# A row layout in runs of 2 KB, loads of row tiles in pairs, and centring shared by VectorE and ScalarE, at the head of a fused attention and gated-MLP kernel

## Chip, cores, metric

One core of a Trainium2 chip. The metric is device time in microseconds (us); medians of several executions are given with their range. Engines: PE is TensorE, DVE is VectorE, ACT is ScalarE, POOL is GpSimd, SP is SyncE, which here only issues DMAs.

## The reference

```python
x  = A_x                                   # (1, 2048, 512) bf16
xn = layernorm(x)                          # over the last axis
q  = (xn @ wq) in 32 heads of 128
o  = softmax(q @ k_cache.T * 128**-0.5) @ v_cache     # 32 heads, 2048 keys
s  = o @ wo                                # (4096 -> 512)
g  = silu((relu(xn @ W_gate) * (xn @ W_up)) @ W_down) # 512 -> 1792 -> 512
out = x + s * g
```

## The kernel before

The program first computes `g`, in four Q blocks of 512 rows, then a long attention stage, then the last projection. The change touches the head of the first Q block only. There the rows are centred (the scale of the layernorm is folded in later), transposed by PE, copied to `xcT`, and multiplied by the first column blocks ("fc", 128 columns) of `W_gate` and `W_up`. The first fc blocks are done row tile by row tile ("small blocks": 4 matmuls of 128 columns for the gate and 4 for up), the others over all 512 rows ("full blocks").

```python
x_t   = x2.rearrange("(n p) d -> p n d", p=128)     # row n*128+p on partition p
out_t = out2.rearrange("(n p) d -> p n d", p=128)
# ... (cut)
FCS = [0, 2, 5, 9, FC]      # W_gate and W_up come in four pieces of fc blocks
HFC = 3                     # so many fc blocks go by row tile
load_x0(sp, 0); load_x0(act, 1)          # single row tiles, 128 KB, 1 KB runs
load_w(sp, Wg_sb, wg_src, sem_wg, 0)     # 256 KB, fc 0 and 1
load_w(act, Wu_sb, wu_src, sem_wu, 0)
load_x0(sp, 2); load_x0(sp, 3)
# pieces 1 of Wg, Wu; second 512 rows of x; pieces 2; pieces 3; third and fourth 512 rows; W_down
_wait(act, eps_tok)
warm_tok = sem_sq.sig(act.activation(sqv[:, 0, :], eps_sb[:], ACTF.Sqrt))   # loads the table
# ... (cut)
def head_center(n):
    atok = ln_aggr([n], ln_stats(n))          # DVE: bn_stats, bn_aggr
    _wait(dve, atok)
    return sem_ln4.sig(dve.tensor_scalar(xc_sb[:, n, :], x_sb[:, n, :], mv[:, n, 0:1], None,
                                         op0=ALU.subtract))
def head_transpose(n, ntok):                  # PE: 4 transposes, then ACT: copy to xcT
    # ... (cut)
def head_ln():
    c0 = head_transpose(0, head_center(0)); warm_mm(4)
    c1 = head_transpose(1, head_center(1))
    n2 = head_center(2); n3 = head_center(3)
    _wait(pe, c0); head_tile(0, 0); head_tile(0, 1)
    _wait(pe, c1); head_tile(1, 0); head_tile(1, 1)
    c2 = head_transpose(2, n2); head_tile(0, 2); head_tile(1, 2)
    # ... (cut)
warm_mm(18); head_ln()      # 18 matmuls on constants while the first loads are under way
```

In the full blocks of the first Q block, DVE also takes the statistics of the later rows of x, one tile per fc block, so it waits there for the later loads of x.

The softmax here doesn't subtract the row's maximum and nothing guards it: scores larger than these inputs give would overflow.

## Time and profile before

| | before |
|---|---|
| time, 6 runs (the prediction had the first 3, median 1286.01) | 1285.68 us (1285.48 to 1286.48) |
| span of the profiled run | 1284.4 us |
| first small block starts | 6.28 us |
| first matmul of the second Q block | 44.03 us |
| from there to the end | 1240.37 us |

Everything after the start of the second Q block is bound by PE. Two lines of the page of the kernel before show it, the busy times by engine and the chain of work that ended last, by engine:

```profile
PE 1279.1 (100%) x12050; PEld 836.4 (65%) x12050; DVE 380.5 (30%) x683; ACT 1002.2 (78%) x1111; POOL 13.2 (1%) x25
...
PE 98%; DVE 1%; ACT 0%; issue 0%; DMA 0%; ACTq 0%; DVEq 0%
```

The timeline of the kernel before, 3 to 7 us. Columns: start in us, busy us, engine, line, operation, output and input, and in brackets how long the engine had stood idle and for whom.

```profile
3.48 0.69 DVE L313 BATCH_NORM_STATS2 stats<-x_sb 128x6 f32<-128x512 bf16 x1 [3.48 <-DMA x_sb<-in_A_x_dram]
...
4.43 0.35 DVE L348 TENSOR_SCALAR xc_sb<-x_sb,mv 128x512 bf16<-128x512 bf16 x1
4.70 0.69 DVE L313 BATCH_NORM_STATS2 stats<-x_sb 128x6 f32<-128x512 bf16 x1
...
4.93 0.38 PE L358 MATMUL ps_acc<-ident,xc_sb 128*128 128x128 bf16 x4 [0.16 <-DVE xc_sb L348]
...
5.64 0.35 DVE L348 TENSOR_SCALAR xc_sb<-x_sb,mv 128x512 bf16<-128x512 bf16 x1
...
6.05 0.40 PE L358 MATMUL ps_acc<-ident,xc_sb 128*128 128x128 bf16 x4 [0.29 <-DVE xc_sb L348]
...
6.28 0.39 PE L410 MATMUL ps_r<-xcT,Wg_sb 128*128 128x128 bf16 x4
```

DVE begins when the first tile has landed, needs 1.2 us a tile, and PE, in order, does tile 1's transposes (6.05) before the first small block (6.28).

The same view at 19 to 22 us:

```profile
19.62 0.69 DVE L313 BATCH_NORM_STATS2 stats<-x_sb 128x6 f32<-128x512 bf16 x1 [0.78 <-DMA x_sb<-in_A_x_dram]
...
19.95 1.03 PE L512 MATMUL ps_r<-xcT,Wu_sb 128*128 128x512 bf16 x4
...
20.51 0.69 DVE L473 TENSOR_TENSOR hT<-gr_sb,ps_r 128x512 bf16<-128x512 bf16 x1
...
21.34 1.02 PE L508 MATMUL ps_r<-xcT,Wg_sb 128*128 128x512 bf16 x4 [0.37 <-DVE hT L473]
```

DVE stood 0.78 us for the third load of x; the product that frees PE's buffer slot came late, and PE's next full block began at 21.34, though the block before it needed PE only to 20.8 (19.95 plus four steps of 0.216).

The DMA view of the kernel before, DMAs in flight around 1 to 1.6 us: what, issuing queue, count, KB each, us from issue to landing.

```profile
Wu_sb<-in_B_W_up_dram ACTq DMA_DIRECT2D x1, 256.0 KB, 4.2
Wg_sb<-in_B_W_gate_dram SPq DMA_DIRECT2D x1, 256.0 KB, 3.9
x_sb<-in_A_x_dram ACTq DMA_DIRECT2D x1, 128.0 KB, 2.9
x_sb<-in_A_x_dram SPq DMA_DIRECT2D x1, 128.0 KB, 2.7
```

The windows view of the kernel before, for PE alone. Columns: stretch, its length, PE busy (instructions), granted clock, DMA share, GB/s.

```profile
1.36:4.77 3.41, 3.41 (x16) 1.00 0.91 248
4.77:8.19 3.42, 2.97 (x48) 1.00 1.09 330
```

Before a first change is recorded the clock column reads 1.00, but PE's pace is then half: the 18 warm-up matmuls took 4.00 us in all, 0.22 each, while eighteen of the same took 2.18 in a4_bridge below, after full speed had been granted. And the stretches are cut by the clock's own record: in this trace full speed was granted at 4.77 us, and the cuts lie there and 3.41 us to either side, the length of the shortest stretch in the changed kernel's record below.

### The profile page before, as it was taken

Reading aid. Unit: us, or ns where it says so; the run is one execution under the profiler, and the core shown is the slowest. Engines: PE = TensorE matmul, PEld = TensorE weight load, DVE = VectorE, ACT = ScalarE, POOL = GpSimd, SP = SyncE. Lnnn points to the kernel's source line nnn. Section 1 sums busy time; section 2 is a strip of 40 time slices with the busy share of each in tenths; the row PEclk is TensorE's granted clock in tenths of the full one; section 3 lists DMA queues with packets and bytes.
Section 4 is the critical chain, followed back from the end, with each engine's and each line's share of the span. In section 5 each row is a group of like instructions: output and inputs, shape, how many; then the busy total and the mean of one; then the engine's idle time right before and its main releaser. Section 6 shows DMA issues by size and latency. Waiting matters only on the chain.

```text
span 1284.4 us, 26956 instructions
## 1 busy us (share of the span) xinstructions
PE 1279.1 (100%) x12050; PEld 836.4 (65%) x12050; DVE 380.5 (30%) x683; ACT 1002.2 (78%) x1111; POOL 13.2 (1%) x25
## 2 busy tenths in 40 slices
PE   9999999999999999999999999999999999999998
PEld 5444466676666666666666666666666666666665
DVE  6433311112222222222222222222222222224355
ACT  3322399998888888888888888888888888888885
POOL 2100000000000000000000000000000000000000
PEclk9999999999999999999999999999999999999999
DMA  9600123332132332332322322233323322332212
GB/s 262 131 1 1 22 46 57 58 55 38 35 54 46 71 54 50 55 70 51 55 43 33 67 46 54 55 66 55 55 51 65 58 35 38 51 67 54 48 16 75
DMA packets 242033, 72.13 MB, mean 56 GB/s; under 512 B 227840, under 2 KB 241920, under 8 KB 241920
## 3 DMA queue, kind: packets, MB, share of 16 engines
q1 hardware_dynamic: 241248, 70.02, 29.6%
q8 instruction: 96, 1.57, 0.5%
q10 hardware_dynamic: 672, 0.39, 0.1%
q14 instruction: 17, 0.14, 0.0%
HBM read 32.77 MB, written 2.10 MB: 27 GB/s over the span
## 4 chain that ended last, share of the span: by engine, by line
PE 98%; DVE 1%; ACT 0%; issue 0%; DMA 0%; ACTq 0%; DVEq 0%
PE ps_acc L769 36%; PE ps_r L664 34%; PE ps_r L597 9%; PE ps_r L618 8%; PE ps_acc L531 3%; PE ps_r L508 3%; PE ps_r L512 3%; PE ps_r L803 1%; DVE stats L313 0%; PE ps_r L410 0%; DVE hT L473 0%; DMA x_sb<-in_A_x_dram 0%; DVE fin_tmp L811 0%; ACT gr_sb L467 0%; DVE x_sb L827 0%
## 5 line engine op out<-in xcount | busy, mean ns | idle before, releaser
L674 ACT ACTIVATE PT<-ps_r 128x1024 bf16<-128x1024 f32 x1024 | 952.5, 1054 | 167.7 <-PE ps_r L664 167.7
L769 PEld LDWEIGHTS ps_acc<-V_sb,PT 128*128 128x128 bf16 x8192 | 621.2, 98 | 241.9 <-ACT PT L674 3.5
L769 PE MATMUL ps_acc<-V_sb,PT 128*128 128x129 bf16 x8192 | 776.7, 220 | 0.0
L664 PE MATMUL ps_r<-QT_sb,KT_sb 128*128 128x512 bf16 x2048 | 754.1, 379 | 0.0
L691 DVE RECIPROCAL rz_sb<-ps_acc 128x4 f32<-128x4 f32 x127 | 23.3, 183 | 729.8 <-PE ps_acc L769 729.8
L664 PEld LDWEIGHTS ps_r<-QT_sb,KT_sb 128*128 128x128 bf16 x2048 | 195.0, 98 | 1.1 <-DVE QT_sb L608 0.4
L597 PE MATMUL ps_r<-xnT,Wq_sb 128*128 128x512 bf16 x512 | 130.9, 379 | 0.0
L618 PE MATMUL ps_r<-Wo_sb,OT_store 128*128 128x512 bf16 x448 | 114.6, 379 | 0.0
L608 DVE CAST QT_sb<-ps_r 128x512 bf16<-128x512 f32 x128 | 88.5, 692 | 48.1 <-PE ps_r L597 48.1
L597 PEld LDWEIGHTS ps_r<-xnT,Wq_sb 128*128 128x128 bf16 x512 | 49.9, 97 | 60.6 <-ACT PT L674 27.1
L694 DVE TENSOR_TENSOR Onorm<-ps_acc,rz_sb 128x512 bf16<-128x512 f32 x127 | 87.8, 691 | 4.4
L618 PEld LDWEIGHTS ps_r<-Wo_sb,OT_store 128*128 128x128 bf16 x448 | 43.8, 98 | 52.9 <-ACT PT L674 0.2
L631 DVE TENSOR_TENSOR s_acc<-s_acc,ps_r 128x512 f32<-128x512 f32 x96 | 66.0, 687 | 17.3 <-PE ps_r L618 17.3
L467 ACT ACTIVATE gr_sb<-ps_r 128x512 bf16<-128x512 f32 x55 | 32.2, 595 | 47.5 <-PE ps_r L508 47.0
L473 DVE TENSOR_TENSOR hT<-gr_sb,ps_r 128x512 bf16<-128x512 bf16 x55 | 37.7, 686 | 47.5 <-PE ps_r L512 41.2
L531 PE MATMUL ps_acc<-Wd_sb,hT 128*128 128x512 bf16 x224 | 49.2, 379 | 0.1
L508 PE MATMUL ps_r<-xnT,Wg_sb 128*128 128x512 bf16 x168 | 43.1, 379 | 0.0
L512 PE MATMUL ps_r<-xnT,Wu_sb 128*128 128x512 bf16 x168 | 43.1, 379 | 0.0
L531 PEld LDWEIGHTS ps_acc<-Wd_sb,hT 128*128 128x128 bf16 x224 | 21.8, 98 | 26.8 <-DVE g_sb L548 0.6
L539 ACT ACTIVATE sig_sb<-ps_acc 128x512 f32<-128x512 f32 x12 | 7.2, 597 | 29.5 <-PE ps_acc L531 29.5
L508 PEld LDWEIGHTS ps_r<-xnT,Wg_sb 128*128 128x128 bf16 x168 | 16.4, 98 | 19.8
L512 PEld LDWEIGHTS ps_r<-xnT,Wu_sb 128*128 128x128 bf16 x168 | 16.4, 98 | 19.8
(56 smaller groups left out, 184.7 us busy)
## 6 DMA issues: line engine op xcount, KB each, us to landing
V_sb<-in_A_v_cache_dram SPq DMA_DIRECT2D x32, 512.0 KB, 4.7
Wq_sb<-in_A_wq_dram SPq DMA_DIRECT2D x32, 128.0 KB, 2.5
Wo_sb<-in_A_wo_dram SPq DMA_DIRECT2D x8, 512.0 KB, 4.8
OT_store<-Onorm SPq DMA_TRANSPOSE x127, 2.5
Wd_sb<-in_B_W_down_dram SPq DMA_DIRECT2D x1, 1792.0 KB, 14.5
x_sb<-in_A_x_dram SPq DMA_DIRECT2D x3, 512.0 KB, 10.8
out_dram<-x_sb SPq DMA_DIRECT2D x6, 256.0 KB, 2.1
Wg_sb<-in_B_W_gate_dram SPq DMA_DIRECT2D x1, 640.0 KB, 10.3
```

Source lines behind the costliest of these rows:

```text
L473: dve.tensor_tensor(hT[par][:, fc, :], gr_sb[gk][:], u_ps, ALU.mult)
L508: ins = pe.matmul(g_ps, Wg_sb[:, c, fs], xT[:, c, xs], start=(c == 0), stop=(c == DC - 1))
L512: ins = pe.matmul(u_ps, Wu_sb[:, c, fs], xT[:, c, xs], start=(c == 0), stop=(c == DC - 1))
L531: ins = pe.matmul(ps_acc[:, jb, 0:D], hT[par][:, fc, j * 128:(j + 1) * 128], Wd_sb[:, fc, :], start=(fc == 0), stop=(fc == FC - 1))
L597: ins = pe.matmul(ps_r[:, bank, :], Wq_sb[b][:, c, :], xnT[:, c, qs], start=(c == 0), stop=(c == DC - 1))
L608: etok = sem_qpe.sig(dve.tensor_copy(QT_sb[b][:, qs], ps_r[:, bank, :]))
L618: ins = pe.matmul(ps_r[:, bank, 0:D], OT_store[g % 2][:, hh, n * 128:(n + 1) * 128], Wo_sb[g % 2][:, hh, :], start=(hh == 0), stop=(hh == ...
L631: dve.tensor_tensor(s_acc[:, n, :], s_acc[:, n, :], ps_r[:, bank, 0:D], ALU.add)
L664: ins = pe.matmul(ps_r[:, 2 * s + tt, :], KT_sb[h % 2][:, t * 128:(t + 1) * 128], QT_sb[h % 2][:, qs], start=True, stop=True)
L674: act.activation(PT[pb][:], ps_r[:, 2 * s:2 * s + 2, :], ACTF.Exp, scale=scale)
L694: dve.tensor_tensor(Onorm[ob][:], o_ap, rz_sb[:].to_broadcast([128, 4, Dh]), ALU.mult))
L769: ins = pe.matmul(o_ap, PT[pb][:, tt, j * 128:(j + 1) * 128], V_sb[vb][:, t, 0:VW], start=(t == 0 and j % 2 == 0), stop=(t == KT - 1 and j ...
```

## The change

The intent: longer runs for the loads of x, both engines at work on the centring, less waiting for late loads, and fewer small blocks. The core of the diff (later helpers and renamings cut):

```diff
-    x_t = x2.rearrange("(n p) d -> p n d", p=128)
-    out_t = out2.rearrange("(n p) d -> p n d", p=128)
+    x_t = x2.rearrange("(p n) d -> p n d", p=128)      # row p*16+n on partition p
+    out_t = out2.rearrange("(p n) d -> p n d", p=128)
-        HFC = 3
+        HFC = 2
-        load_x0(sp, 0)
-        load_x0(act, 1)
+        load_x0(0)                     # tiles 0,1 in one DMA: 2 KB runs, all on SP's queue
+        load_x0(1)                     # tiles 2,3
         load_w(sp, Wg_sb, wg_src, sem_wg, 0)
+        _wait(act, eps_tok)
+        sem_sq.sig(act.activation(sqv[:, 0, :], eps_sb[:], ACTF.Sqrt))
         load_w(act, Wu_sb, wu_src, sem_wu, 0)
-        load_x0(sp, 2)
-        load_x0(sp, 3)
 ... (pieces 1, second 512 rows of x, pieces 2)
+        load_xq(2)                     # third 512 rows of x, ahead of the last pieces
         load_w(sp, Wg_sb, wg_src, sem_wg, 3)
         load_w(sp, Wu_sb, wu_src, sem_wu, 3)
-        for Q in range(2, QB):
+        for Q in range(3, QB):
             load_xq(Q)
+        def center_act(n):
+            _wait(act, x0_tok[n // 2])
+            stok = sem_xa.sig(act.activation(xc_sb[:, n, :], x_sb[:, n, :], ACTF.Copy,
+                                             scale=-1.0 / D, accum_out=nmean[:, n, :]))
+            _wait(act, stok)
+            return sem_xa.sig(act.activation(xc_sb[:, n, :], x_sb[:, n, :], ACTF.Identity,
+                                             bias=nmean[:, n, :]))
         def head_ln():
-            c0 = head_transpose(0, head_center(0))
-            warm_mm(4)
-            c1 = head_transpose(1, head_center(1))
+            n0 = center_dve(0)
+            n1 = center_act(1)
+            p0 = head_tr(0, n0)
+            p1 = head_tr(1, n1)
+            warm_mm(3)
+            c0 = head_copy(0, p0, act)
+            stok = ln_stats(2)          # DVE: statistics of tile 2, then tile 1's copy
+            c1 = head_copy(1, p1, dve)
 ... (tile 2 centred by DVE, tile 3 by ACT; copies 2 by DVE, 3 by ACT; small blocks of fc 0 and 1;
      the statistics of tiles 1 and 3 come last)
```

More of the change, by code (lines that the diff above doesn't have):

```diff
@@ L142, in bass_recurrent_scan__mha_block_cached__glu_gated_reglu__prompt_kernel @@
         xcT = SB_([128, DC, NQ], BF16, "xcT")
+        nmean = SB_([128, 4, 1], F32, "nmean")
         r2 = SB_([128, 4, 1], F32, "r2")
@@ L157, in bass_recurrent_scan__mha_block_cached__glu_gated_reglu__prompt_kernel @@
         sem_x = [newsem(16) for _ in range(QB)]
-        sem_x0 = [newsem(16) for _ in range(4)]
+        sem_x0 = [newsem(16) for _ in range(2)]
         sem_wg = [newsem(16) for _ in range(4)]
@@ L224, in bass_recurrent_scan__mha_block_cached__glu_gated_reglu__prompt_kernel, with load_x0 @@
         x_tok = {}
-        def load_x0(eng, n):
-            x0_tok[n] = sem_x0[n].sig(eng.dma_start(x_sb[:, n:n + 1, :], x_t[:, n:n + 1, :]))
+        def load_x0(k):
+            x0_tok[k] = sem_x0[k].sig(
+                sp.dma_start(x_sb[:, 2 * k:2 * k + 2, :], x_t[:, 2 * k:2 * k + 2, :]))
         def load_xq(Q):
@@ L243, in bass_recurrent_scan__mha_block_cached__glu_gated_reglu__prompt_kernel @@
         load_w(sp, Wu_sb, wu_src, sem_wu, 2)
+        load_xq(2)
         load_w(sp, Wg_sb, wg_src, sem_wg, 3)
         load_w(sp, Wu_sb, wu_src, sem_wu, 3)
-        for Q in range(2, QB):
+        for Q in range(3, QB):
             load_xq(Q)
         sem_wd.sig(sp.dma_start(Wd_sb[:], B_W_down.rearrange("(c p) d -> p c d", p=128)))
-        _wait(act, eps_tok)
-        warm_tok = sem_sq.sig(act.activation(sqv[:, 0, :], eps_sb[:], ACTF.Sqrt))
         def issue_kt(h):
@@ L309, in ln_stats @@
             if n < 4:
-                _wait(dve, x0_tok[n])
+                _wait(dve, x0_tok[n // 2])
             elif n % 4 == 0:
@@ L342, in bass_recurrent_scan__mha_block_cached__glu_gated_reglu__prompt_kernel, with center_dve, head_tr @@
         xt_ready = {Q: [] for Q in range(QB)}
-        def head_center(n):
-            atok = ln_aggr([n], ln_stats(n))
-            _wait(dve, atok)
+        def center_dve(n):
+            _wait(dve, ln_aggr([n], ln_stats(n)))
             return sem_ln4.sig(
                 dve.tensor_scalar(xc_sb[:, n, :], x_sb[:, n, :], mv[:, n, 0:1], None, op0=ALU.subtract))
-        def head_transpose(n, ntok):
+        def center_act(n):
+            _wait(act, x0_tok[n // 2])
+            stok = sem_xa.sig(
+                act.activation(xc_sb[:, n, :], x_sb[:, n, :], ACTF.Copy, scale=-1.0 / D,
+                               accum_out=nmean[:, n, :]))
+            _wait(act, stok)
+            return sem_xa.sig(
+                act.activation(xc_sb[:, n, :], x_sb[:, n, :], ACTF.Identity, bias=nmean[:, n, :]))
+        def head_tr(n, ntok):
             tp_ps = acc_bf[n % 2]
@@ L359, in head_transpose, with head_copy @@
                                    xc_sb[:, n, c * 128:(c + 1) * 128], ident[:])
-            ptok = sem_tp.sig(ins)
-            src = tp_ps[:, 0:DC * 128].rearrange("p (c q) -> p c q", c=DC)
-            _wait(act, ptok)
-            acc_free[n % 2] = sem_xa.sig(act.copy(xcT[:, :, n * 128:(n + 1) * 128], src))
+            return sem_tp.sig(ins)
+        def head_copy(n, ptok, eng):
+            src = acc_bf[n % 2][:, 0:DC * 128].rearrange("p (c q) -> p c q", c=DC)
+            _wait(eng, ptok)
+            copy, sem = (act.copy, sem_xa) if eng is act else (dve.tensor_copy, sem_xt)
+            acc_free[n % 2] = sem.sig(copy(xcT[:, :, n * 128:(n + 1) * 128], src))
             return acc_free[n % 2]
@@ L373, in head_ln @@
         def head_ln():
-            c0 = head_transpose(0, head_center(0))
-            warm_mm(4)
-            c1 = head_transpose(1, head_center(1))
-            n2 = head_center(2)
-            n3 = head_center(3)
+            n0 = center_dve(0)
[6 more added lines that the diff above has]
+            c1 = head_copy(1, p1, dve)
+            _wait(dve, ln_aggr([2], stok))
+            n2 = sem_ln4.sig(
+                dve.tensor_scalar(xc_sb[:, 2, :], x_sb[:, 2, :], mv[:, 2, 0:1], None, op0=ALU.subtract))
+            n3 = center_act(3)
             _wait(pe, c0)
@@ L383, in head_ln @@
             head_tile(1, 0)
+            p2 = head_tr(2, n2)
+            c2 = head_copy(2, p2, dve)
             head_tile(1, 1)
-            c2 = head_transpose(2, n2)
-            head_tile(0, 2)
-            head_tile(1, 2)
+            p3 = head_tr(3, n3)
+            c3 = head_copy(3, p3, act)
             _wait(pe, c2)
             head_tile(2, 0)
-            c3 = head_transpose(3, n3)
             head_tile(2, 1)
-            head_tile(2, 2)
             _wait(pe, c3)
-            for fc in range(HFC):
-                head_tile(3, fc)
+            head_tile(3, 0)
+            head_tile(3, 1)
+            for n in (1, 3):
+                ln_aggr([n], ln_stats(n))
         half_slots = []
```

## The prediction

> **What bounds the kernel.** The page gives PE 1279.1 of 1284.4 us busy; the chain that ended last is 98% PE. By the windows view PE never idles from 38 us to the last ten. The change leaves that work as it is and can only move when PE gets through the first 38 us. There the timeline shows:
> - 0 to 6.28 us: warm-up and transposes; the first useful matmul (xcT, row tile 0) starts at 6.28. PE, in order, waited for tile 1: DVE takes the tiles in turn, 1.2 us each (statistics 0.69, aggregate 0.18, centring 0.35).
> - 6.28 to 12.18: 12 small blocks (0.445 us) and two transposes (0.22): 5.78 us of work in 5.90.
> - 12.18 to 37.97: 11 full blocks (1.73) and 28 down matmuls (0.216): 25.07 us of work in 25.79. Of the 0.72 lost, 0.5 is at 20.8, where DVE had stood 0.78 us for the third load of x (landed 10.8 us after issue) and freed a slot late; 0.2 at 37.8, where the first gate (r2h, table load 1.28, tanh 0.69, two DVE steps) frees its bank late.
>
> **What the change does.**
> - x in pairs, 2 KB runs, same bytes. The first pair lands near 3.5 us (before: 3.46 and 3.63); the second, now ahead of Wg, near 4.3. The third load of x goes ahead of the last 1.28 MB of weights: at the trace's 349 GB/s 3.7 us earlier, so DVE's wait goes.
> - ACT issues the first Wu load after table load and warm-up, near 2.2 us (was 1.16). It took 4.2 us to land; again so, it lands at 6.2 to 6.4, just when needed. [...] the trace agrees (from 4 to 5 us the queues show 62 and 52%), so Wu need not wait for all of SP's.
> - ACT centres tile 1 in two passes, estimated 0.6 us each from its 0.58 to 0.60 for 512 columns: done near 4.85, as tile 0. Both transposed by 5.4; copy ends near 6.0, first useful matmul 6.05: gain 0.2.
> - Tile 2's copy goes to DVE (estimated 0.69 from its PSUM reads; ACT 0.58), and one small block and one transpose less stand between its transpose and its use: 1.2 us needed, 0.9 covered, loses 0.3.
> - HFC 3 to 2: four small blocks (1.78) become one full (1.73), and an early wait for the second Wu piece goes: gains 0.15.
> - Two late statistics (1.7 us) fall where DVE has room.
> - Output writes become 2 KB for early pairs: off the chain.
>
> **Sum.** Start +0.2; tile-2 bubble -0.3; Wu late -0.15 (0 to 0.4); small blocks +0.15; wait at 20.8 +0.5; gate wait +0.2, since DVE is no longer behind: 0.6 us gained, carried to the end because PE is bound there.
>
> **Prediction: 1285.4 us, range 1284.7 to 1286.1** (before 1286.01, runs 0.8 apart). Chances: faster by over 2% 0.01; within 2% 0.98; slower 0.01.
>
> **What would show it.** Timeline: first small block near 6.05; a PE gap near 8.3 before tile 2's blocks; DVE never waiting for x after the start; no PE gap at 20 to 21 or at 37; the second Q block's first matmul 0.6 earlier than 44.03, all later work shifted alike.
>
> **What would make it wrong.** Reads with a 16 KB stride between partitions landing later than contiguous ones; Wu landing after 6.5; the accumulating ACT pass costing much over 0.6; DVE still behind, so the gate wait remains; exp and matmuls falling differently in step in the long stage.

Between 4 and 5 us the packets of SP's and ACT's queues took 52 and 62% of the 16 engines' time. The sum: its six terms (+0.2, -0.3, -0.15, +0.15, +0.5, +0.2) come to 0.6 us.

## More of the kernel before

The three sets of experiments ran on three chips (a runs, b runs, c runs); the kernel before, timed beside each, agreed within 0.05 us.

Wg was issued at 1.19 and landed near 5.1; the weights are there before PE wants them.

## The result, and the profile after

| | before | changed |
|---|---|---|
| time, 6 runs each | 1285.68 us (1285.48 to 1286.48) | 1287.67 us (1285.70 to 1289.55) |
| ratio | | 1.0014, interval 1.0001 to 1.0027 |
| span of the profiled run | 1284.4 | 1288.2 |
| first small block | 6.28 | 8.18 |
| second Q block | 44.03 | 47.83 |
| from there to the end | 1240.37 | 1240.40 |

A ratio is the mean time of one kernel's fast runs over the mean of the other's fast runs of the same rounds, so it is not quite the ratio of the medians. At a limit of 2% the two kernels count as the same; what follows is about effects under 0.4%, read from the traces and, where it is said, from runs that do not overlap. "Within 2%" was right; the sign and the range (1284.7 to 1286.1) were wrong, and the runs spread over 3.9 us. The profiled run is the slowest of the six, so it shows the loss at its largest.

The two lines of the page of the changed kernel:

```profile
PE 1281.0 (99%) x12025; PEld 838.3 (65%) x12025; DVE 380.2 (30%) x683; ACT 1004.2 (78%) x1115; POOL 13.2 (1%) x25
...
PE 99%; DMA 0%; DVE 0%; issue 0%; SPq 0%
```

The chain is PE to 99% here as well, so the page alone hides the loss. The timeline of the changed kernel, 3 to 9 us:

```profile
3.98 0.63 ACT L353 ACTIVATE xc_sb<-x_sb 128x512 bf16<-128x512 bf16 x1 [1.75 <-DMA x_sb<-in_A_x_dram]
3.98 0.70 DVE L314 BATCH_NORM_STATS2 stats<-x_sb 128x6 f32<-128x512 bf16 x1 [3.98 <-DMA x_sb<-in_A_x_dram]
...
4.52 0.19 ACT L353 ACTIVATION_READ_ACCUMULATOR xc_sb<-x_sb 128x1 f32 x1
...
4.74 0.72 ACT L357 ACTIVATE xc_sb<-x_sb,nmean 128x512 bf16<-128x512 bf16 x1
4.93 0.35 DVE L348 TENSOR_SCALAR xc_sb<-x_sb,mv 128x512 bf16<-128x512 bf16 x1
...
5.43 0.61 PE L367 MATMUL ps_acc<-ident,xc_sb 128*128 128x128 bf16 x8 [1.02 <-DVE xc_sb L348]
...
6.08 0.42 DVE L375 COPY xcT<-ps_acc 128x512 bf16<-128x512 bf16 x1 [0.19 <-PE ps_acc L367]
...
8.18 0.58 PE L430 MATMUL ps_r<-xcT,Wg_sb 128*128 128x128 bf16 x4 [1.81 <-DMA Wg_sb<-in_B_W_gate_dram]
...
8.56 0.63 PE L430 MATMUL ps_r<-xcT,Wu_sb 128*128 128x128 bf16 x4
```

DVE and ACT begin at 3.98, half a microsecond later than DVE did before. The transposes come at 5.43. Then PE stands 1.81 us until 8.18, and the waits view of the changed kernel (who waited for whom: us in total, times, longest) names the DMA:

```profile
PE ps_r L430 <- DMA Wg_sb<-in_B_W_gate_dram: 1.8, 1, 1.8
PE ps_acc L367 <- DVE xc_sb L348: 1.0, 1, 1.0
```

The DMA view of the changed kernel, DMAs in flight at 1.5 to 2.1 us, shows the landing that PE waited for: Wg was issued at 1.66 and took 6.4 us.

```profile
x_sb<-in_A_x_dram SPq DMA_DIRECT2D x1, 256.0 KB, 3.7
Wu_sb<-in_B_W_up_dram ACTq DMA_DIRECT2D x1, 256.0 KB, 6.3
Wg_sb<-in_B_W_gate_dram SPq DMA_DIRECT2D x1, 256.0 KB, 6.4
```

The small blocks themselves are slow: the gate's four matmuls took 0.58 and the next group began 0.38 later (later ones 0.43), where the step was 0.22 before. The windows view for PE, cut at the changes of the clock's record (3.89, 7.31 and 14.13) and at steps of 3.41 us from them, shows the clock at half:

```profile
0.48:3.89 3.41, 3.12 (x15) 1.00 0.52 139
3.89:7.31 3.42, 1.46 (x16) 1.00 0.97 299
7.31:10.72 3.41, 2.54 (x25) 0.50 1.07 365
10.72:14.13 3.41, 3.41 (x35) 0.50 1.07 369
14.13:17.54 3.41, 3.41 (x30) 1.00 1.08 371
```

In the stretch from 3.89 to 7.31 PE was busy 1.46 of 3.42 us. At its end the clock was halved. The next stretch held 2.54 us of work, and the clock stayed halved through the one after it, 6.83 us in all; from 14.13 it was full again.

So the 3.80 us between the two second Q blocks can be split, by arithmetic, with the table's starts and one number that the experiments give. (Against the second trace of the kernel before, b0_before, the parts differ: its stretch is 37.36.) With full clock and no wait the change's work from first small block to second Q block takes 36.85 us (five runs below show 36.84 to 36.86); here it took 39.65, so the halved clock cost 2.80. Before, the same stretch took 37.75, so the change's own gain there is 0.90. The later start costs 1.90. 1.90 + 2.80 - 0.90 = 3.80.

### The profile page after: what moved, and what is told of

Same layout as the page of the kernel before. It is cut to its first block, busy times and chain, and to the rows that moved or that the text cites. A ratio compares the mean times of both kernels' runs of the same rounds, so it can differ in the third digit from the quotient of the medians.

```text
span 1288.2 us, 26910 instructions
## 1 busy us (share of the span) xinstructions
PE 1281.0 (99%) x12025; PEld 838.3 (65%) x12025; DVE 380.2 (30%) x683; ACT 1004.2 (78%) x1115; POOL 13.2 (1%) x25
## 4 chain that ended last, share of the span: by engine, by line
PE 99%; DMA 0%; DVE 0%; issue 0%; SPq 0%
PE ps_acc L789 36%; PE ps_r L684 34%; PE ps_r L617 9%; PE ps_r L638 8%; PE ps_acc L551 4%; PE ps_r L528 4%; PE ps_r L532 4%; PE ps_r L823 1%; DMA Wg_sb<-in_B_W_gate_dram 0%; PE ps_r L430 0%; DVE fin_tmp L831 0%; DVE x_sb L847 0%; PE ps_acc L532 0%; PE ps_acc L528 0%; PE ps_acc L367 0%
```

## Experiments

Eleven runs followed, two of them (a1_same, b0_before) of kernels already seen, all correct; each timed kernel had five executions. The trace records 16 landings for each of the early loads, called its shares below. In the kernel before, those of the first x DMA came from 3.09 to 3.46 us and DVE began on that tile at 3.48, after the last; in the changed kernel those of Wg came from 5.93 to 8.04 and PE began at 8.18. The table uses this: "spread" is from first to last of the 16.

| run | first x DMA: last share (spread) | first Wg: median, last share | first small block | from it to second Q block | second Q block | time, us |
|---|---|---|---|---|---|---|
| before | 3.46 (0.37) | 4.65, 5.06 | 6.28 | 37.75 | 44.03 | 1285.68 (1285.48 to 1286.48) |
| b0_before | 3.52 (0.34) | 4.63, 4.88 | 6.58 | 37.36 | 43.94 | one run, 1285.63 |
| changed | 3.96 (0.94) | 6.29, 8.04 | 8.18 | 39.65 | 47.83 | 1287.67 (1285.70 to 1289.55) |
| a1_same | 4.05 (1.07) | 6.03, 6.85 | 6.99 | 36.84 | 43.83 | 1285.91 (1285.57 to 1288.97) |
| a2_rowlayout | 3.58 (0.34) | 6.25, 7.36 | 7.50 | 38.43 | 45.93 | 1285.84 (1285.50 to 1287.65) |
| a3_layout_only | 4.08 (0.96) | 5.30, 5.75 | 7.21 | 38.04 | 45.25 | 1286.28 (1285.58 to 1286.96) |
| a4_bridge | 3.95 (1.00) | 6.40, 8.03 | 8.16 | 36.85 | 45.01 | 1286.85 (1286.35 to 1287.19) |
| b1_wg_second | 4.17 (0.94) | 4.61, 5.02 | 6.70 | 37.11 | 43.81 | 1285.57 (1285.38 to 1287.06) |
| b3_old_loads | 3.43 (0.49) | 4.60, 5.11 | 6.17 | 36.86 | 43.03 | 1284.70 (1284.60 to 1284.78) |
| b4_xq2_early | 3.64 (0.35) | 5.15, 5.34 | 6.48 | 36.89 | 43.37 | 1285.12 (1285.05 to 1285.59) |
| c1_row_wg_second | 3.68 (0.46) | 4.45, 4.60 | 6.21 | 37.63 | 43.84 | 1286.05 (1285.53 to 1286.68) |
| c2_old_loads_new_layout | 4.50 (1.30) | 5.42, 6.16 | 7.03 | 36.86 | 43.89 | 1285.14 (1285.13 to 1285.68) |
| c3_x_first | 3.28 (0.44) | 5.75, 6.50 | 6.64 | 36.84 | 43.48 | 1285.02 (1284.71 to 1285.31) |

The columns from "first x DMA" to "second Q block" are of the one profiled run. The profiled execution was the slowest of its five in a2_rowlayout (1287.65) and a3_layout_only (1286.96), one of the two slow ones in c2_old_loads_new_layout (1285.60) and one of the two fast ones in c1_row_wg_second (1285.56). In every trace the rest, from the second Q block to the end, is 1240.35 to 1240.40 us: nothing after the head, the stores in the new layout included, moves the time. The kernel before, run beside the experiments, had medians of 1285.66, 1285.69 and 1285.64 in the three sets.

### a1_same: the changed kernel again

No edit.

> The changed kernel unaltered, to see whether the first profile is typical. Theory: its time follows the landing of the first Wg piece (8.1 us in the first profile) and what the clock then does; so runs spread from about 1285.5 to 1289.5, mean near 1287.5, and the profile's delay at the second Q block equals its total delay. If the first profile was a rare accident: all runs near 1285.4.

Measured: 1285.91, ratio 1.0006 (0.9994 to 1.0019). Four runs lie at 1285.57 to 1286.11 and one at 1288.97. The spread is the kernel's, but its middle was lower than expected: over all eleven runs of the changed kernel the median is 1286.43. This profile was of the fastest run. Its waits view and its windows (cut at its first grant of full speed, 3.84, and at steps of 3.41 us) stand against those of the first:

```profile
PE ps_r L430 <- DMA Wg_sb<-in_B_W_gate_dram: 0.5, 1, 0.5
```

```profile
3.84:7.25 3.41, 1.75 (x21) 1.00 1.05 318
7.25:10.66 3.41, 3.41 (x65) 1.00 1.07 368
```

Wg's last share landed at 6.85, not 8.04. PE waited 0.5 us, was busy 1.75 of 3.41 us in the stretch after its first grant, and kept its clock (1.00 in the next). The later start (+0.71) was paid by the change's gain (0.91): second Q block at 43.83, 0.20 before the old one. The same program thus reaches its second Q block anywhere from level with the kernel before to 3.80 us behind it.

### a2_rowlayout: the old row layout in the changed kernel

```diff
-    x_t = x2.rearrange("(p n) d -> p n d", p=128)
+    x_t = x2.rearrange("(n p) d -> p n d", p=128)     # and out_t alike
```

> Changed kernel with rows laid out as before (row n*128+p on partition p) in load and store; all the rest of the change kept, pairs now in 1 KB runs. Layout theory: the first Wg piece lands by 6.0 us, the 16 shares of each early load lie within 0.5 us, no idle PE, clock stays full, 1285.0 to 1285.6 with a small spread. Rival (order of loads: 512 KB of x ahead of Wg in one queue): Wg still lands near 8, time 1287 to 1289 as in the changed kernel. Rival (late issue of Wu by ScalarE): Wu lands after Wg and PE waits for it.

Measured: 1285.84, ratio 1.0002 (0.9989 to 1.0016), range to 1287.65. The layout theory was half right: x landed early and together (spread 0.34), but Wg did not; its last share came at 7.36, and the clock was halved from 7.50 to 10.91:

```profile
4.08:7.50 3.42, 1.36 (x16) 1.00 0.95 286
7.50:10.91 3.41, 3.41 (x33) 0.50 1.09 348
10.91:14.32 3.41, 3.41 (x48) 1.00 1.10 350
```

The waits view names ACT for the wait before the first block, but that block starts 0.14 after Wg's last share, as in both profiles of the changed kernel. So the layout is not the whole cause. What is left of the new loads (the order, the pairs, one queue) has a part; this run does not say which. Wu's last share came at 6.18, before Wg's: the late issue of Wu was not the trouble here.

### a3_layout_only: the new row layout alone in the kernel before

```diff
-    x_t = x2.rearrange("(n p) d -> p n d", p=128)
+    x_t = x2.rearrange("(p n) d -> p n d", p=128)     # and out_t alike
```

> Kernel before with only the new row layout (tiles still load singly, 1 KB runs at a 16 KB stride). Layout theory: x lands late and scattered, first Wg piece late (over 6.5 us), PE idles, clock may fall: 1286.5 to 1290. Rival (order): 1285.7 as before.

Measured: 1286.28, ratio 1.0004 (0.9992 to 1.0017). x landed scattered (spread 0.96) and late, as the layout theory had it; Wg landed in time (5.75), against it. The first block came at 7.21. In this trace the first full grant of the clock came only at 9.62 us: the small blocks' matmul groups began 0.43 us apart before it and 0.23 after. Of the two stretches of 3.41 us before the grant, the first

```profile
2.79:6.20 3.41, 2.63 (x16) 1.00 1.03 310
```

held 2.63 us of work and the second 3.42; that 2.63 was too little for an earlier grant is inference. The 1.00 of that line is the missing record again, not a full clock.

### a4_bridge: more warm-up work in the gap

```diff
-            warm_mm(3)
+            warm_mm(18)      # PE busy while it would wait for Wg
```

> Changed kernel with 18 instead of 3 warm-up matmuls after the first transposes (15 x 0.107 = 1.6 us more PE work, in order, before the first small block), so that PE has no idle stretch while it waits for Wg. Clock theory: granted clock stays full from about 4.2 us, small blocks 0.445 us each; when Wg lands at 8.1 the delay of the second Q block against before is 0.9 to 1.5 us, not 3.8: all runs near 1286.5 to 1287.3, with a smaller spread than the changed kernel. Rival (clock falls anyway, or the half-speed blocks have another cause): blocks still at 0.85 us and 1288 or more.

Measured: 1286.85, all five runs within 0.84 us. By luck Wg's last share came at 8.03, as in the first profile of the changed kernel (8.04), and the first block at 8.16 (8.18). The windows of this run and its first small block:

```profile
1.98:5.39 3.41, 2.79 (x14) 1.00 0.77 226
5.39:8.80 3.41, 3.26 (x38) 1.00 1.05 338
```

```profile
8.16 0.38 PE L430 MATMUL ps_r<-xcT,Wg_sb 128*128 128x128 bf16 x4
```

PE kept its full clock, the block's four matmuls took 0.38 instead of 0.58, and the stretch to the second Q block took 36.85 instead of 39.65. With the start alike, the clock is 2.80 us. (The longer warm-up itself ran until 8.04, so in this kernel it holds the first block back even where Wg lands early.) That the added work kept the clock, and not something else in this execution, is likely but not shown by this trace alone: without the 15 added matmuls (1.6 us) the stretch from 5.39 would have held about 1.6 us, an estimate from its 3.26, which lies between 1.46 (clock lost) and 1.75 (kept). The narrow spread of all five runs speaks for the added work. The second Q block came 0.98 after that of the kernel before, inside the expected 0.9 to 1.5. As a version it is no gain: its fastest run, 1286.35, is slower than all nine runs of the kernel before (to 1286.15).

### b0_before: the kernel before, for a second trace

> The kernel before, once more, for a second trace of its early loads. If the narrow landing of the first profile is its rule: the 16 shares of each early x and weight load land within 0.5 us, first Wg by 6.1 us. If it was luck: spreads of 1 us and more here too, Wg after 6.5.

Measured: 1285.63 (one run). The narrow landings came again: x spread 0.34, Wg's last share at 4.88, Wu's at 5.42. Wg's own spread (0.73, and 0.88 in the first trace) is wider than the 0.5 expected. The first block came 0.30 later than in the first trace, the second Q block 0.09 earlier: a later start cost this kernel nothing here; DVE waited 0.5 us for the third load of x instead of 0.8.

### b1_wg_second: Wg between the pairs, new layout

```diff
         load_x0(0)
-        load_x0(1)
         load_w(sp, Wg_sb, wg_src, sem_wg, 0)
+        load_x0(1)
```

> Changed kernel, the first Wg piece issued between the two pairs of x instead of after both; new row layout kept. Order theory: the median share of Wg lands about 0.7 us earlier (near 5.8 instead of 6.3 to 6.6) and the last one before 7; PE's wait for Wg shrinks to under 0.5 us, no fall of the clock in most runs, median 1285.2 to 1285.7. Layout theory alone (scatter of the 16 shares comes from the 16 KB stride): the last share of Wg still 1 to 2 us behind the median, and runs spread up to 1288.

Measured: 1285.57, ratio 1.0001 (0.9988 to 1.0013), range to 1287.06. Wg's last share came at 5.02 instead of 6.85 to 8.04, so the order is a cause of Wg's lateness. But now Wu was late (median 6.16, last 7.12, spread 1.97): PE's first Wu matmuls began at 7.17, 0.47 after the first Wg matmuls instead of 0.22, so this wait cost 0.25. And x was scattered as in all runs with the new layout (0.94).

### b3_old_loads: all of the change but its early loads

```diff
-        load_x0(0)
-        load_x0(1)
+        load_x0(sp, 0)        # single tiles, old row layout
+        load_x0(act, 1)
         load_w(sp, Wg_sb, wg_src, sem_wg, 0)
-        _wait(act, eps_tok)   # ... and the Sqrt, now after the loads
         load_w(act, Wu_sb, wu_src, sem_wu, 0)
+        load_x0(sp, 2)
+        load_x0(sp, 3)
```

> All of the change's arithmetic and PE order (ScalarE centring, HFC 2, third x load earlier), with the old early loads: old row layout, four single tiles over two queues, Wg and Wu second in their queues. If the loads alone cost the gain: first small block at 6.1 to 6.4 us, no wait for Wg, clock full from its first grant, second Q block's first matmul near 43.1, 1284.6 to 1285.2 in all runs (0.6 to 1.0 under the kernel before). Rival (ScalarE's centring itself starts PE late): first block at 6.8 or later and time as before.

Measured: 1284.70, five runs within 0.18 us, ratio 0.9991 (0.9979 to 1.0004). The interval includes 1, but the slowest of the five (1284.78) is under the fastest of the nine runs of the kernel before (1285.38), and the second Q block comes at 43.03, exactly 1.00 us earlier than in the first trace. Its timeline for PE:

```profile
4.90 0.95 PE L368 MATMUL ps_acc<-ident,xc_sb 128*128 128x128 bf16 x8
...
6.17 0.40 PE L431 MATMUL ps_r<-xcT,Wg_sb 128*128 128x128 bf16 x4
```

The centring on ACT is not what starts PE late: the rival falls. This version beats both kernels in these runs.

### b4_xq2_early: one load moved in the kernel before

```diff
+        load_xq(2)
         load_w(sp, Wg_sb, wg_src, sem_wg, 3)
         load_w(sp, Wu_sb, wu_src, sem_wu, 3)
-        for Q in range(2, QB):
+        for Q in range(3, QB):
```

> Kernel before with one edit: the third load of x ahead of the last weight pieces. Prediction's terms: the 0.5 us at 20.8 and 0.2 at 37.8 vanish, second Q block near 43.4, time 0.5 to 0.7 under the kernel before (1285.0 to 1285.2). Rival: the wait only moves (the last weights now come late, or DVE stays behind): time within 0.2 of before.

Measured: 1285.12, ratio 0.9996 (0.9982 to 1.0010); the medians differ by 0.57. The second Q block comes at 43.37. The stretch from the first small block takes 36.89, as in b3_old_loads (36.86): this single line gives nearly all of what the change gains after the start, counted from the first trace (37.75; from b0_before's 37.36 the gain is 0.47). The rest of b3's gain is its earlier start, 6.17 against 6.48.

### c1_row_wg_second: Wg between the pairs, old layout

The edit of b1_wg_second made in a2_rowlayout.

> Old row layout, pairs kept on one queue, but the first Wg piece between the pairs and Wu still issued by ScalarE after its table load. If the order of Wg behind 512 KB of x was the second cause of the late weights: x spread under 0.5 us, Wg by 5.5, Wu by 6.3, first small block at 6.2 to 6.5, all runs 1284.6 to 1285.1. If pairs or the late Wu issue are to blame: last share of Wu or Wg at 6.8 or later, runs to 1286 and more.

Measured: 1286.05, ratio 1.0003 (0.9990 to 1.0015). The landings were as the order theory wanted (x spread 0.46, Wg 4.60, Wu 5.64), and the first block came at 6.21, as expected; the time was not. The timeline shows a wait that nobody had named:

```profile
6.70 0.69 DVE L314 BATCH_NORM_STATS2 stats<-x_sb 128x6 f32<-128x512 bf16 x1 [1.69 <-DMA x_sb<-in_A_x_dram]
...
7.31 0.41 DVE L375 COPY xcT<-ps_acc 128x512 bf16<-128x512 bf16 x1
...
7.77 0.40 PE L430 MATMUL ps_r<-xcT,Wg_sb 128*128 128x128 bf16 x4 [0.49 <-DVE xcT L375]
```

The second pair of x now landed late (6.67). DVE's order has the statistics of tile 2 ahead of tile 1's copy, so the copy waited for data that it does not need, and PE stood 0.49 us for the copy. (This profile is of a fast run, 1285.56; what made the others slower is not seen.) In this change, then, the pair has to come early for DVE's order and Wg has to come early for PE, on one queue.

### c2_old_loads_new_layout: the layout alone in the fastest version

b3_old_loads with the row layout of the change, for x and the output.

> The fastest version so far (old early loads) with only the row layout changed to the new one; single tiles become 1 KB runs at a 16 KB stride. Layout theory: the shares of the first x tiles spread about 1 us instead of 0.5, centring starts 0.4 us later, PE idles about that much longer; 1285.0 to 1286.5, with a wider spread of runs. Rival (order of the loads alone): 1284.7 as the fastest version.

Measured: 1285.14 (five runs, 1285.13 to 1285.68; ratio to the kernel before 0.9997, 0.9984 to 1.0011) against 1284.70 for b3_old_loads: 0.44 us, with no run in common. x spreads over 1.30 us, the last share comes 1.07 later than in b3_old_loads, the first block 0.86 later, and the stretch from there is the same 36.86. The two were timed in different sets, on different chips, beside a kernel before of 1285.69 and 1285.64. The profile is of one of the two slow runs (1285.60), so its 0.86 is more than the median loses. The rival falls: the layout costs by itself.

### c3_x_first: the order alone in the fastest version

```diff
         load_x0(act, 1)
-        load_w(sp, Wg_sb, wg_src, sem_wg, 0)
-        load_w(act, Wu_sb, wu_src, sem_wu, 0)
         load_x0(sp, 2)
         load_x0(sp, 3)
+        load_w(sp, Wg_sb, wg_src, sem_wg, 0)
+        load_w(act, Wu_sb, wu_src, sem_wu, 0)
```

(ACT's queue keeps its order; only Wg moves, behind tiles 2 and 3.)

> The fastest version with only the first Wg piece moved behind tiles 2 and 3 of x on its queue (x before weights, as in the changed kernel; old row layout). Order theory: Wg's last share lands 0.5 to 0.9 us later (6.2 to 6.6 instead of about 5.4), small blocks start up to 0.4 later, 1284.8 to 1285.2. If this order by itself scatters the shares as in the run with pairs in the old layout: last share of Wg over 7, runs to 1287.

Measured: 1285.02 (ratio to the kernel before 0.9995, 0.9983 to 1.0008) against 1284.70 for b3_old_loads: 0.32 us, though one of its five runs (1284.71) is as fast. Wg's last share came at 6.50 instead of 5.11 (more than expected: the median moved by 1.15, the spread was 0.97), and the first block 0.47 later. The order costs by itself too, by less than the layout and, with one run of five as fast, less surely (again across two sets).

## Why the prediction was wrong

Point by point, as the prediction put it:

- "can only move when PE gets through the first 38 us": right. The rest is 1240.37 us before and 1240.40 after, and 1240.35 to 1240.40 in all traces.
- "The first pair lands near 3.5 us" and the second "near 4.3": wrong, 3.96 and 4.85 in the first profile. Only bytes and issue times were counted. In six traces with the new layout the first x DMA's shares spread over 0.94 to 1.30 us; in seven with the old one over 0.34 to 0.49. c2_old_loads_new_layout shows the cost of the layout alone: 0.44 us. The prediction had named strided reads as a way to be wrong, and gave them no time in the sum.
- **"Start +0.2": the step that failed.** It took Wg's landing for granted. The early loads were costed for x and for Wu; the first Wg, which now stands behind 512 KB of x instead of 128 KB, had no term. It landed at 6.85 to 8.04 in three traces of this loading order, and the first block came at 6.99 to 8.18: not 0.2 gained but 0.7 to 1.9 lost. The late x had its part: in the first profile ACT's copy of tile 0 to `xcT` ended at 6.43, not near 6.0, so by x alone the block would have started about 0.4 later than predicted (an estimate); the wait for Wg added some 1.7 in that profile and 0.5 in a1_same. c3_x_first shows the order alone: 0.32 us.
- "ACT issues the first Wu load after table load and warm-up, near 2.2 us", "lands at 6.2 to 6.4", "Wu late -0.15": the issue was wrong, it went out at 1.54, while the table load ran until 2.01 and the Sqrt ahead of it in the program started at 2.02. The landing was wrong too, the other way: 7.84, 6.62 and 7.79 in the three traces of this loading order. "Wu landing after 6.5" was on the prediction's own list of what would make it wrong, and it came true. It hardly showed while Wg came later still; in the first profile, with Wu landing 0.20 ahead of Wg, an early Wg alone would not have saved the start, and in b1_wg_second, where Wg was early, Wu cost 0.25.
- A term was missing from the sum altogether: the clock. In the first profile PE was busy 1.46 of 3.42 us, its clock was halved after that for 6.83 us, and 2.80 us of that profile's loss are that (a4_bridge, same start, full clock). The other recorded fall lasted 3.41 us (a2_rowlayout), and the first grants of full speed came from 3.84 to 9.62 us after the start; what sets these times was not shown. With the landing of Wg the clock accounts for the two profiles of the same program, 1285.57 us (no fall) and 1289.55. That it gives the spread of the other nine runs was the author's guess: the mean granted clock listed for the runs of 1289.06 and 1288.97 us is 1.000, against 0.997 for the one of 1289.55 (a late first grant does not show in that mean: the profiled run of a3_layout_only lists 1.000 too).
- "Tile 2's copy goes to DVE (estimated 0.69)", "loses 0.3": wrong, harmless. DVE's copy took 0.42, and in a1_same tile 2's first block started 0.02 after the transposes ahead of it were through.
- ACT's two passes "0.6 us each": 0.63 and 0.72, plus 0.19 to read the accumulator. Tile 1 was ready as tile 0 was, within 0.2 us: near enough.
- "Wait at 20.8 +0.5; gate wait +0.2", "HFC ... gains 0.15": the sum, 0.85, is right; the stretch shrank by 0.91 in a1_same. Its parts were off: moving the third load of x gives 0.86 of it (b4_xq2_early), so the smaller HFC and the rest of the new order give about 0.05. That the sum fits is in part luck: it is counted from the first trace, and from b0_before's the same stretch shrank by only 0.5.

The gain was therefore there and was given back ahead of it, by loads. With the old early loads the change is worth 0.99 us by the medians (1285.69 to 1284.70), more than the 0.6 predicted.

Not all of the loss is taken apart. The changed kernel's median over eleven runs (1286.43) is 1.73 us above b3_old_loads; the layout alone (0.44) and the order alone (0.32) make 0.76 of it. The rest lies in how they act together, with the pairs, the single queue and the clock, and no run separates these.

What stays open: why strided runs land scattered (the changed kernel's trace shows packets of 2 KB that took up to 0.95 us, usually 0.08, but not where they stood); why in the changed kernel's order single shares of Wu and Wg come 0.8 to 2 us after their median, even in the old layout (once there, the lag stays: in the first profile the five DMAs that follow the first Wg on SP's queue spread over 2.06 to 2.13 us each); whether pairs as such, rather than the order, add to that; and why four of the first six runs were over 1287 and one of the next five. With one profile per kernel, the landings of the other runs are not seen.

## What to carry to other kernels

When a change reorders the first loads, give every load that PE's first instructions need its own landing time, measured by its last share, and look at the slowest; a load moved ahead can move another back (c3_x_first, with two tiles of x ahead of it: Wg's last share at 6.50 instead of 5.11). When PE will stand idle early, cost the clock as well: here the same lateness cost 0.98 us with PE kept busy and 3.80 without. Take a second profile before explaining a spread: the first one here was the slowest of eleven runs.

## Figures of the hardware that these traces give

- PE's clock, one trace each: after a stretch with PE busy 1.46 of 3.42 us, which held a gap of 1.02 and the first half of one of 1.81, it was halved (changed kernel, 3.89 to 7.31 us); so it was after one with 1.36 (a2_rowlayout, 4.08 to 7.50); after one with 1.75 it stayed full (a1_same, 3.84 to 7.25). From half speed, stretches with 2.54 (changed kernel, 7.31 to 10.72) and 2.63 us (a3_layout_only, 2.79 to 6.20) were followed by another at half speed, one with 2.75 (b1_wg_second, 2.02 to 5.44) by full speed. These are single cases and no limits; busy times are the profile's, transposes counted.
- The scatter of a DMA's 16 shares: 0.34 to 0.49 us for 128 to 256 KB of contiguous rows at the kernel's start (seven traces), 0.94 to 1.30 for the same bytes in runs 16 KB apart (six traces), up to 2.1 for the first Wg queued behind them (changed kernel, 5.93 to 8.04).
- The accumulator output of an ACT pass: a separate instruction of 0.19 us at the end of a pass of 0.63, 0.73 for both (3.98 to 4.71 in the changed kernel).
